# One V tile near the end of a decode step loaded as three row groups instead of one

## The chip, the cores and the metric

The kernel runs on one core of one Trainium2 chip. The core has five instruction streams that matter here: TensorE (PE in the profile, with its weight loads as PEld), VectorE (DVE), ScalarE (ACT), GpSimd (POOL) and SyncE (SP). SyncE issues nearly all transfers; sixteen DMA engines carry them out. The metric is the device time of one execution in microseconds (us). Three timed runs of the kernel before gave 1319.47, 1320.37 and 1320.67 us, so the median is 1320.37 us.

## What is computed

One decode step of a transformer block, two batch entries with one new token each: a layer norm, attention of 32 heads against a cache of 8192 keys and values per head, a residual, a second layer norm, a gated feed-forward network (SwiGLU), and a second residual. All numbers are float32. Cut to what matters, with D = 512, H = 32, Dh = 128, Sk = 8192, F = 1792:

```python
q = (layernorm(x) @ wq).reshape(B, Sq, H, Dh).transpose(0, 2, 1, 3)
scores = einsum("bhqd,bhkd->bhqk", q, k_cache) * Dh ** -0.5
o = einsum("bhqk,bhkd->bhqd", softmax(scores), v_cache)
h = x + o.transpose(0, 2, 1, 3).reshape(B, Sq, H * Dh) @ wo
n = layernorm(h)
out = h + (silu(n @ w_gate) * (n @ w_up)) @ w_down
```

The cache makes up nearly all of the data: 64 pairs of batch entry and head, each with 4 MB of K and 4 MB of V, which is 537 MB of the 565 MB that the kernel reads. Each byte of it is used once.

## The kernel before

**Tiles.** The 64 pairs are numbered i = 2 * head + batch, so NP = 64. A K or V of one pair, 8192 rows of 128 numbers, is laid on the 128 partitions of the on-chip memory so that partition p holds cache rows 64p to 64p + 63: 32 KB in one run per partition. Such a tile is called an item. All items, and the weights too, go through one ring of five buffers of that size (RING = 5).

**The list of loads.** `order` is a list written out before anything is issued. For each pair it has K of that pair and the V's that are due (`after[i]`; V runs behind K, by one pair at first and by five at the end), with wq and wo between them. Behind the last K (pair 63) come V of 58, V of 59, 60 and 61, the last part of wo, V of 62, V of 63 in four pieces, then w_gate, w_up in two pieces and w_down in four (8, 4, 1 and 1 of its 14 column blocks). `NP - 6` is pair 58: the first V behind the last K.

**Issuing.** `pump()` goes down the list and calls `load()` for each piece as soon as the item five places before it in the ring has been used. The `dma_start` at line 120 issues the K and V pieces, line 130 wo, line 136 w_gate and w_up, line 141 w_down, all on SyncE's queue. Each load waits on SyncE until its buffer is free: V of 58 takes the buffer of K of 61, wo's last part that of K of 63, V of 62 that of V of 58.

**Work on a K.** VectorE multiplies the K tile by the broadcast q in two halves (line 245), sums each product over the 128 numbers (line 248), and takes the maximum of its partition (line 256). PE and ScalarE then make the softmax weights `p` (lines 260 to 281).

**Work on a V.** `pv` (line 288) runs 32 matmuls whose stationary side is four columns of `p` and whose moving side is 512 columns of the V tile, so each reads all 128 partitions; it cannot start before the whole tile is there. `epilogue` (lines 301 to 311) folds the result into `oT`, and `project_o` (line 318) multiplies by wo.

**The end.** After V of 63 come the residual `h` (line 376), the layer norm, the gate and up products (line 396), their product `gu` and its transpose `gT` (lines 414 and 420), and 56 matmuls with w_down (line 425, recorded as 112 passes), which read the column blocks of w_down in order. `res` (line 434) is copied out and two small transfers of four rows each store it (line 436), one issued by SyncE and one by ScalarE. The input x is loaded by ScalarE as two rows (line 64).

Of the kernel before, what the change touches and what calls it, by code (L numbers as in the profile page):

```python
# [13 lines left out]
P = 128  # L14
# [5 lines left out]
def tile_decode_block(  # L20
# [12 lines left out]
    nc = tc.nc  # L33
    B, _, D = x.shape
    _, H, S, DH = k_cache.shape
# [10 lines left out]
    NP = B * H  # L46
# [23 lines left out]
    def k_pieces(i):  # L70
        return NCH if i == 0 else 1
# [32 lines left out]
        stream_v(v)  # L104
    order += [(("wg", 0), 0, DC)] + [(("wu", 0), c, 2) for c in range(0, DC, 2)]
    order += [(("wd", 0), c, n) for c, n in ((0, 8), (8, 4), (12, 1), (13, 1))]
    items = list(dict.fromkeys(o[0] for o in order))
    slot = {}
    done = set()
# [2 lines left out]
    def load(item, e, n):  # L112
        if item not in slot:
            slot[item] = ring.tile([P, NJ * DH], F32, name="ring")
        t = slot[item]
        kind, i = item
        if kind in "kv":
            src = k_cache if kind == "k" else v_cache
            h, b = divmod(i, B)
            nc.sync.dma_start(  # L120
                t[:, e * DH : (e + n) * DH],
                src[b, h].rearrange("(p j) d -> p (j d)", p=P)[:, e * DH : (e + n) * DH],
            )
        elif kind == "wq":
            nc.sync.dma_start(
                t[:, : DC * G * DH].rearrange("p (c m) -> p c m", c=DC),
                wq[:, i * G * DH : (i + 1) * G * DH].rearrange("(c p) m -> p c m", p=P),
            )
        elif kind == "wo":
            nc.sync.dma_start(  # L130
                t[:, : G * D].rearrange("p (c m) -> p c m", c=G),
                wo[i * G * DH : (i + 1) * G * DH, :].rearrange("(c p) m -> p c m", p=P),
            )
        elif kind in ("wg", "wu"):
            src = w_gate if kind == "wg" else w_up
            nc.sync.dma_start(
                t[:, e * F : (e + n) * F],
                src.rearrange("(p c) f -> p (c f)", p=P)[:, e * F : (e + n) * F],
            )
        else:  # L140
            nc.sync.dma_start(
                t[:, e * D : (e + n) * D],
                w_down.rearrange("(p c) m -> p (c m)", p=P)[:, e * D : (e + n) * D],
            )

    def pump():
        while state["next"] < len(order):
            piece = order[state["next"]]
            if piece[0] not in slot:
                n = items.index(piece[0])  # L150
                if n >= RING and items[n - RING] not in done:
                    return
            load(*piece)
            state["next"] += 1
# [16 lines left out]
    for n in range(2):  # L171
        t = psum.tile([P, W * DH], F32, name=f"opart{n}")
# [160 lines left out]
    for i in range(NP):  # L333
        n = FINE if k_pieces(i) > 1 else 2 * FINE
# [142 lines left out]
```

## Time and profile before

| what | value |
|---|---|
| median of three timed runs | 1320.37 us (1319.47 to 1320.67) |
| the profiled execution's own time | 1320.22 us |
| its span, first to last instruction | 1318.4 us |
| VectorE busy | 1156.2 us, 88% of the span |
| PE busy | 649.3 us, 49% |
| ScalarE busy | 117.3 us, 9% |
| read from the cache and weights | 564.66 MB, 428 GB/s over the span |
| share of the closing chain put down to DMA | 45% |
| share of the closing chain put down to VectorE | 47% |

The profile is one execution. Its span leaves out 1.8 us of the execution's own time, which lie before the first and after the last instruction. The chain of work that ended last is followed back from the last instruction, at each step to whatever released it. A DMA's "issue to landing" runs from the instruction on the issuing engine to the last of its completions: each DMA engine that takes part in a transfer writes a completion packet of 4 bytes behind its own data, and a waiting engine goes on when all are in. The views count these packets among those under 512 B.

### The profile page before, as it was taken

The page shows a single profiled execution, that of the slowest core. Times are in us where ns is not written, and L with a number is a line of the kernel's source. Part 1 is how long each engine was busy: PE and PEld are TensorE (multiplying, and loading weights), DVE is VectorE, ACT ScalarE, POOL GpSimd, SP SyncE. Part 2 cuts the span into 40 slices and gives each one's busy share as a digit, 9 for nine tenths or more (in the row PEclk, how much of TensorE's full clock was granted, in tenths as well). Part 3 has the DMA queues.
Part 4 walks back from the last instruction along what each step waited for, and adds up shares of the span by engine and source line. Part 5 has one row for each costly group of instructions (what it writes and reads, how often), then busy time and mean ns, then how long its engine had stood idle before and what let it go on. Part 6 is the DMA issues. An engine that isn't in the chain of part 4 may idle for free.

```text
span 1318.4 us, 8048 instructions
## 1 busy us (share of the span) xinstructions
PE 649.3 (49%) x3328; PEld 251.2 (19%) x3328; DVE 1156.2 (88%) x474; ACT 117.3 (9%) x404; POOL 1.9 (0%) x9
## 2 busy tenths in 40 slices
PE   5444544247554435535653454442644754454585
PEld 2111111013212111211221122111212211111122
DVE  6999999997999999989889999997799999999601
ACT  1001000001000100000100000000100000100010
POOL 0000000000000000000000000000000000000000
PEclk9666666677675756666867656666856766666697
DMA  9999999999999999999999999999999999999997
GB/s 404 437 431 428 433 437 433 423 437 432 428 436 435 430 430 435 437 429 429 433 429 434 435 429 431 433 432 435 431 432 426 430 437 432 433 429 435 434 422 327
DMA packets 26633, 565.19 MB, mean 429 GB/s; under 512 B 2394, under 2 KB 2402, under 8 KB 8804
## 3 DMA queue, kind: packets, MB, share of 16 engines
q1 hardware_dynamic: 26584, 564.67, 99.6%
q8 instruction: 26, 0.43, 0.1%
q14 instruction: 11, 0.09, 0.0%
q10 hardware_dynamic: 12, 0.01, 0.0%
HBM read 564.66 MB, written 0.00 MB: 428 GB/s over the span
## 4 chain that ended last, share of the span: by engine, by line
DVE 47%; DMA 45%; PE 7%; issue 0%; ACT 0%; DVEq 0%
DMA ring<-in_A_k_cache_dram 31%; DVE s L248 24%; DVE ring L245 22%; DMA ring<-in_A_v_cache_dram 12%; PE wide L223 4%; DMA ring<-in_B_w_down_dram 2%; PE opart L288 2%; PE attn L318 1%; DMA ring<-in_A_wq_dram 1%; DVE m L256 0%; PE small L425 0%; PE small L304 0%; DVE r L279 0%; PE small L260 0%; DVE gm L264 0%
## 5 line engine op out<-in xcount | busy, mean ns | idle before, releaser
L245 DVE TENSOR_TENSOR ring<-ring,qsb 128x4096 f32<-128x4096 f32 (+1 forms) x130 | 565.4, 4349 | 69.2 <-DMA ring<-in_A_k_cache_dram 56.8
L248 DVE TENSOR_REDUCE s<-ring 128x32 f32<-128x4096 f32 (+1 forms) x130 | 565.0, 4347 | 0.7 <-DVE gm L264 0.5
L288 PE MATMUL opart<-ring,p 128*4 128x512 f32 x2048 | 349.5, 843 | 111.3 <-DMA ring<-in_A_v_cache_dram 111.1
L260 PE MATMUL small<-ident,m 128*1 128x128 f32 x128 | 30.4, 328 | 276.5 <-DVE m L256 276.5
L266 PE MATMUL small<-gm,nscale 1*128 1x1 f32 x128 | 35.8, 346 | 207.7 <-DVE gm L264 207.7
L288 PEld LDWEIGHTS opart<-ring,p 128*4 128x4 f32 x2048 | 57.6, 107 | 346.5 <-issue 228.5
L304 PE MATMUL small<-rdiag,osb 128*128 128x1 f32 x512 | 94.1, 305 | 7.1 <-ACT osb L301 7.1
L304 PEld LDWEIGHTS small<-rdiag,osb 128*128 128x128 f32 x512 | 88.7, 261 | 31.2 <-issue 17.4
L266 PEld LDWEIGHTS small<-gm,nscale 1*128 1x128 f32 x128 | 30.3, 292 | 217.6 <-DVE gm L264 214.9
L260 PEld LDWEIGHTS small<-ident,m 128*1 128x1 f32 x128 | 5.5, 81 | 332.9 <-DVE m L256 330.6
L223 PE MATMUL wide<-ring,xb 128*128 128x512 f32 x128 | 58.4, 616 | 2.9 <-DMA ring<-in_A_wq_dram 2.9
L281 ACT ACTIVATE rdiag<-diag,r 128x4 f32<-128x4 f32 x64 | 19.0, 297 | 451.4 <-DVE r L279 451.4
L275 PE MATMUL small<-rs,ones 128*128 128x1 f32 x128 | 36.1, 351 | 46.9 <-ACT p L271 46.9
L264 DVE TENSOR_REDUCE gm<-small 1x1 f32<-1x128 f32 x64 | 17.4, 272 | 34.1 <-PE small L260 34.1
L301 ACT ACTIVATE osb<-opart 128x512 f32<-128x512 f32 x64 | 37.8, 590 | 88.9 <-PE opart L288 88.8
L275 PEld LDWEIGHTS small<-rs,ones 128*128 128x128 f32 x128 | 30.6, 297 | 52.4 <-ACT p L271 52.4
L268 ACT ACTIVATE nb<-small 128x1 f32<-128x1 f32 x64 | 11.0, 172 | 290.4 <-PE small L266 290.0
L318 PE MATMUL attn<-ring,oT 128*2 128x512 f32 x64 | 36.7, 734 | 0.3 <-ACT oT L311 0.3
L311 ACT ACTIVATE oT<-small 128x1 f32<-128x1 f32 x64 | 11.0, 171 | 277.3 <-PE small L304 277.3
L223 PEld LDWEIGHTS wide<-ring,xb 128*128 128x128 f32 x128 | 24.9, 197 | 35.8 <-issue 35.8
L376 DVE TENSOR_TENSOR h<-attn,xs 2x512 f32<-2x512 f32 x1 | 0.7, 678 | 30.5 <-PE attn L318 30.5
L271 ACT ACTIVATE p<-s,nb 128x64 f32<-128x64 f32 x64 | 22.2, 347 | 2.1
(43 smaller groups left out, 87.7 us busy)
## 6 DMA issues: line engine op xcount, KB each, us to landing
ring<-in_A_k_cache_dram SPq DMA_DIRECT2D x63, 4096.0 KB, 31.4
ring<-in_A_v_cache_dram SPq DMA_DIRECT2D x63, 4096.0 KB, 30.5
ring<-in_A_wq_dram SPq DMA_DIRECT2D x4, 2048.0 KB, 21.4
ring<-in_A_wo_dram SPq DMA_DIRECT2D x4, 2048.0 KB, 27.9
ring<-in_A_k_cache_dram SPq DMA_DIRECT2D x4, 1024.0 KB, 12.3
ring<-in_A_v_cache_dram SPq DMA_DIRECT2D x4, 1024.0 KB, 22.3
ring<-in_B_w_gate_dram SPq DMA_DIRECT2D x1, 3584.0 KB
ring<-in_B_w_up_dram SPq DMA_DIRECT2D x2, 1792.0 KB, 37.2
```

The costliest lines, as they stand in the source:

```text
L223: nc.tensor.matmul(ps, xb[:, c * B + b, :], w[:, c, n : n + 512], start=(c == 0), stop=(c == DC - 1),)
L245: nc.vector.tensor_tensor(kt, kt, qb, op=OP.mult)
L248: nc.vector.tensor_reduce(st[i]["s"][:, j0 : j0 + n], k_view(i, j0, n), axis=AX.X, op=OP.add)
L260: nc.tensor.matmul(st[i]["mrow"], st[i]["m"], ident, start=True, stop=True)
L266: nc.tensor.matmul(nb_ps, nscale, gm, start=True, stop=True)
L271: nc.scalar.activation(st[i]["p"], st[i]["s"], AF.Exp, bias=nb, scale=SCALE, accum_out=rs)
L275: nc.tensor.matmul(st[i]["den"], ones, rs, start=True, stop=True)
L281: nc.scalar.activation(st[i]["r"], diag, AF.Copy, scale=r)
L288: nc.tensor.matmul(o[32 * t : 32 * t + W, :], st[i]["p"][:, w * W : (w + 1) * W], vt[:, w * W * DH : (w + 1) * W * DH], start=(w < 4), sto ...
L301: nc.scalar.activation(osb, opart[i % 2], AF.Copy)
L304: nc.tensor.matmul(ot_ps, osb[:, a * DH : (a + 1) * DH], st[i]["r"][:, a : a + 1], start=(a == 0), stop=(a == W - 1),)
L318: nc.tensor.matmul(attn, oT[:, h, :], w[:, h - g * G, :], start=(h == 0), stop=(h == H - 1))
```

## The change

The list `order`, the ring and all work on the tiles stay as they are. V of pair 58 is issued as three transfers in a row on SyncE's queue instead of one: rows (partitions) 0 to 111, rows 112 to 119 and rows 120 to 127, each with the full 32 KB per row. Together they fill the same buffer with the same bytes. The matmuls that read the tile depend on all three. All other K and V loads still run the loop once, over 128 rows.

```diff
     order += [(("wd", 0), c, n) for c, n in ((0, 8), (8, 4), (12, 1), (13, 1))]
+
+    SHARED = ((0, 112), (112, 8), (120, 8))
+    shared = {("v", NP - 6)}
     items = list(dict.fromkeys(o[0] for o in order))
...
             h, b = divmod(i, B)
-            nc.sync.dma_start(
-                t[:, e * DH : (e + n) * DH],
-                src[b, h].rearrange("(p j) d -> p (j d)", p=P)[:, e * DH : (e + n) * DH],
-            )
+            rows = src[b, h].rearrange("(p j) d -> p (j d)", p=P)
+            for r0, nr in SHARED if item in shared else ((0, P),):
+                nc.sync.dma_start(
+                    t[r0 : r0 + nr, e * DH : (e + n) * DH],
+                    rows[r0 : r0 + nr, e * DH : (e + n) * DH],
+                )
```

## The prediction

> **What bounds the kernel now.** I begin with the page's row of the DMA engines in 40 slices and with its table of queues (packets, MB, share of sixteen engines' time).
>
> ```profile
> DMA  9999999999999999999999999999999999999997
> ...
> q1 hardware_dynamic: 26584, 564.67, 99.6%
> q8 instruction: 26, 0.43, 0.1%
> q14 instruction: 11, 0.09, 0.0%
> q10 hardware_dynamic: 12, 0.01, 0.0%
> ```
>
> All sixteen engines are busy until the last slice. Nearly all of it is queue q1, SyncE's loads; beside it run 37 fetches of program code (q8 and q14). Next comes the view by stretches of time, whose last two columns are the DMA share and GB/s: first a long steady stretch, then the end cut finely.
>
> ```profile
> 120.00:1200.00 1080.00, 520.19 (x2572) 202.18 (x2564) 1004.94 (x393) 95.64 (x341) 0.00 (x0) 0.66 1.00 432
> ...
> 1296.00:1307.00 11.00, 8.54 (x74) 2.38 (x73) 0.79 (x2) 0.54 (x1) 0.00 (x0) 0.81 1.01 429
> ...
> 1309.20:1310.20 1.00, 0.00 (x0) 0.00 (x0) 0.00 (x0) 0.00 (x0) 0.00 (x0) 0.50 0.64 270
> ...
> 1310.40:1312.00 1.60, 1.60 (x32) 1.60 (x36) 0.00 (x0) 0.00 (x0) 0.00 (x0) 0.50 0.54 215
> 1312.00:1312.60 0.60, 0.60 (x20) 0.60 (x16) 0.00 (x0) 0.00 (x0) 0.00 (x0) 0.50 0.22 82
> 1312.60:1313.50 0.90, 0.90 (x24) 0.90 (x20) 0.00 (x0) 0.00 (x0) 0.00 (x0) 0.50 0.06 25
> 1313.50:1313.90 0.40, 0.40 (x20) 0.40 (x16) 0.00 (x0) 0.00 (x0) 0.00 (x0) 0.83 0.01 5
> ```
>
> The steady rate is 432 GB/s, 27.0 per engine, so one row of 32,768 bytes occupies an engine for 32,768 / 27.0e3 = **1.21 us**. That is the change's unit. The end shows that the sixteen do not finish together. A share of 0.64 is ten engines of sixteen, so six are done by 1309.2; 0.54 is nine, so a seventh ends near 1310.2; eight end between 1312.0 and 1312.6; 0.06 is one, and it ends at about 1313.6. Every engine has the same loads, so the late nine are late by something else. The spread is there already at the V in question, whose sixteen completions (the packets under 512 B) fall into three neighbouring windows, 1229.05 to 1230.3, to 1231.7 and to 1233.1:
>
> ```profile
> DMA packets 23, 0.56 MB, mean 446 GB/s; under 512 B 6, under 2 KB 6, under 8 KB 6
> ...
> DMA packets 23, 0.69 MB, mean 492 GB/s; under 512 B 2, under 2 KB 2, under 8 KB 2
> ...
> DMA packets 29, 0.69 MB, mean 492 GB/s; under 512 B 8, under 2 KB 8, under 8 KB 8
> ```
>
> Six, two, eight: a spread of 4 us between first and last engine. Code fetches are the likely cause: 26 fetches of 16 KB that always fall on the same engines push these back. Last, the chain of work that ended last, from the end of the K work on (start, length, what):
>
> ```profile
> 1222.14 55.33 DMA ring<-in_A_v_cache_dram x2
> 1277.52 3.66 PE opart L288 x32
> 1281.19 29.07 DMA ring<-in_B_w_down_dram
> 1310.39 4.86 PE small L425 x112
> 1315.28 0.29 DVE res L434
> ```
>
> The last 93 us are transfers with two short PE pieces between them. w_down's first piece lands at 1281.19 + 29.07 = 1310.26, PE starts at 1310.39 and runs without a stop to 1315.25, so its other three pieces are in time. **The end is set by the slowest of sixteen engines at w_down's first piece.** That engine has 1313.6 - 1310.26 = 3.3 us of load behind it. The others have the same behind theirs, so they have that piece in 3.3 us before they end: the eight at 1308.7 to 1309.3, the seventh at 1306.9, the six by 1305.9.
>
> **The change part by part.** *Issue.* SyncE's timeline around the load has these rows:
>
> ```profile
> 1202.68 0.80 SPq L120 DMA_DIRECT2D ring<-in_A_v_cache_dram  x2
> ...
> 1222.14 0.80 SPq L120 DMA_DIRECT2D ring<-in_A_v_cache_dram  x2
> ```
>
> V of 58 and V of 59 are issued within 0.80 us, then SyncE waits until 1222.14 for a buffer. Two more issues at about 0.4 us each end near 1204.3. V of 59, the only load queued behind them, comes 0.8 us later, and its data are not due before 1229, when V of 58's first completions come. Price nothing; without that cover 0.8 us.
>
> *Wait.* The 32 matmuls of V of 58 now wait for three transfers.
>
> ```profile
> 1233.39 6.15 PE L288 MATMUL opart<-ring,p 128*4 128x512 f32 x32 [3.12 <-DMA ring<-in_A_v_cache_dram]
> ...
> 1241.47 0.38 SPq L130 DMA_DIRECT2D ring<-in_A_wo_dram  x1
> 1241.94 17.54 SPq L120 DMA_DIRECT2D ring<-in_A_v_cache_dram  x1
> ...
> 1243.18 6.37 PE L288 MATMUL opart<-ring,p 128*4 128x512 f32 x32 [1.86 <-DMA ring<-in_A_v_cache_dram]
> ```
>
> Behind them on PE stand pair 58's epilogue and V of 59's matmuls (1243.18), and on SyncE the load of V of 62, which takes V of 58's buffer. That load's issue is held 17.54 us with its engines full of earlier work. A landing some microseconds later than 1233 makes V of 62's issue begin later inside that hold, and moves V of 59's matmuls by a little; the next thing the transfers wait for is far off. Price nothing; that cover would be gone only for a delay of over ten microseconds.
>
> *Rows per engine.* 128 rows on sixteen engines are eight each, 112 are seven. How a load of fewer rows than engines is split shows in q10: it carries x's two rows and one store of four rows, and its 12 packets are just (2 + 2) + (4 + 4), one data packet and one completion for each row, so one engine for each row. An eight-row load then occupies eight engines, with one row each. Two of them on the same eight give these 7 + 1 + 1 = nine rows and leave the others with seven: **eight engines gain 1.21 us of work and eight lose 1.21 us.** All engines are full to the end, so the shift stays until w_down.
>
> The single-packet records behind the views, which no view prints, put x's two rows on engines of the early group; if the engines are always filled from the same end, the eight that gain work are mostly the early ones. [...]
>
> *Sum.* The early ones are seven, and the half that gains has eight, so one of the nine late engines is in it too. The very last, if it is in the half that loses, has w_down's first piece at 1310.26 - 1.21 = 1309.05. The late one in the half that gains has it at 1308.7 to 1309.3 plus 1.21, so 1309.9 to 1310.5: it takes over the end. The change comes to **-0.4 to +0.2 us; I take -0.1**. More than 1.3 us cannot be had in any case, since the other operand is not ready earlier:
>
> ```profile
> 1308.38 0.65 DVE L420 STREAM_TRANSPOSE gT<-gu 128x448 f32<-128x448 f32 x1
> ```
>
> It ends at 1309.03 against PE's start at 1310.39.
>
> *Unknown: several engines at neighbouring rows.* In a load of 128 rows each engine has rows of its own; in the short ones eight engines write eight neighbouring rows at once, and none of the rows above shows such writes. [...] If each engine keeps its rate, nothing. [...] I take nothing, nearest to the steady row, where 432 GB/s hold over 1080 us, and keep the other end as a rival.
>
> **Rivals.** [...]
>
> [...]
>
> *Wrong half.* If the eight that gain hold the last engine, w_down's first piece lands at 1310.26 + 1.21: +1.2, **1321.6 us**. For it: the views do not number the engines. Against it: x's two rows.
>
> *It does not do what it says.* If the short loads are spread so that each engine still gets the same bytes, nothing moves: **1320.4 us**. Against it: the twelve packets of q10.
>
> **How the numbers follow.** The sum is made against the profiled execution, 1320.22 us with a span of 1318.4; the median of the runs shown is 1320.37, 0.15 above it, and I move that median. Forecast: 1320.37 - 0.1 = 1320.3 us, its own range 1319.9 to 1320.6. Two runs of this kernel can be told apart from about 0.2%, 2.6 us. Chances: the forecast 0.42; shared way 0.40, of which 0.27 lies beyond +2.6; wrong half 0.08; nothing moved 0.05; a mishap in issue or waits that costs over 2.6 us 0.02; a gain of over 2.6 us, which the operand gT excludes by all I see, 0.03. So faster 0.03, same 0.42 + 0.13 + 0.08 + 0.05 = 0.68, slower 0.27 + 0.02 = 0.29. The range goes from 1319.3 (the forecast's lower end less the spread of the runs) to 1324.8 (the shared way up to +4.4), leaving out about one in ten.
>
> **What would show it.** V of 58 with 48 completions less the unused ones (16 + 8 + 8 = 32 packets) confirms the split. Forecast right: w_down's first piece lands within 0.5 us of 1310.3, the six early engines end 1.2 us later, most of the late eight 1.2 us earlier, so the step in the DMA share near 1312 moves to about 1311. [...] Wrong half: the last engine ends near 1314.8. I am wrong altogether if the end no longer hangs on w_down's first piece, or if engines stand idle before 1308.

## The result, and the profile after

The changed kernel took 1335.19 us (median of four runs, 1334.64 to 1336.48) against 1319.96 us for the kernel before (median of four: the three runs above and one more). The ratio is 1.0115 with a 95% interval of 1.0102 to 1.0127: **15.2 us slower**. The forecast was 1320.3 us and its range ended at 1324.8. Both are far off.

The page of the changed kernel, rows of the DMA engines and queues, in the same 40 slices:

```profile
span 1334.7 us, 8052 instructions
...
DMA  9999999999999999999999999999999999999997
GB/s 408 427 438 431 432 435 429 436 428 438 424 438 427 439 428 436 429 435 428 436 426 437 430 434 437 428 435 430 436 429 431 433 432 432 435 429 340 316 426 325
DMA packets 26649, 565.19 MB, mean 423 GB/s; under 512 B 2410, under 2 KB 2418, under 8 KB 8820
...
q1 hardware_dynamic: 26600, 564.67, 99.6%
```

The engines are as busy as before, but in slices 37 and 38 they move 340 and 316 GB/s instead of some 430. The bytes are the same. The profiled execution is the slowest of the four (1336.48 us), 16.3 us above the profiled one of the kernel before. Queue q1 has 26,600 packets against 26,584, sixteen more: V of 58 now has 16 + 8 + 8 completions instead of 16, so the split is carried out as intended. Where the rate falls is seen in the view by stretches (the last two columns are DMA share and GB/s). First the kernel before:

```profile
1218.00:1224.00 6.00, 3.00 (x26) 1.25 (x18) 4.63 (x3) 0.84 (x3) 0.00 (x0) 0.99 1.01 437
1224.00:1235.00 11.00, 2.77 (x12) 1.25 (x16) 11.00 (x4) 0.61 (x3) 0.00 (x0) 0.54 0.99 429
1235.00:1251.00 16.00, 12.68 (x75) 3.43 (x67) 6.66 (x4) 1.66 (x4) 0.00 (x0) 0.68 1.01 433
1251.00:1300.00 49.00, 36.02 (x217) 10.92 (x221) 2.82 (x8) 5.53 (x15) 0.54 (x1) 0.83 1.01 427
```

The same stretches of the changed kernel:

```profile
1218.00:1224.00 6.00, 2.35 (x22) 1.11 (x14) 4.32 (x2) 0.82 (x3) 0.00 (x0) 0.97 1.08 273
1224.00:1235.00 11.00, 1.16 (x4) 0.99 (x4) 6.88 (x3) 0.61 (x3) 0.00 (x0) 0.50 1.03 220
1235.00:1251.00 16.00, 0.00 (x0) 0.00 (x0) 11.08 (x5) 0.30 (x1) 0.00 (x0) 0.50 0.97 203
1251.00:1300.00 49.00, 37.12 (x213) 10.40 (x213) 0.45 (x2) 5.95 (x15) 0.00 (x0) 0.83 1.00 425
```

For 33 us, 1218 to 1251, the sixteen engines run at **half rate with a full busy share**, and then at full rate again. In these 33 us they move 437 x 6 + 429 x 11 + 433 x 16 = 14.3 MB before and 273 x 6 + 220 x 11 + 203 x 16 = 7.3 MB after. The missing 7.0 MB take 16.1 us at 432 GB/s, and the span grew by 16.3, from 1318.4 to 1334.7. That is nearly the whole loss of this execution.

The slow stretch reaches loads that were not touched. VectorE's timeline at the first half of K of 63, whose load was issued ahead of V of 58, shows how long it had to wait in the kernel before

```profile
1223.71 4.42 DVE L245 TENSOR_TENSOR ring<-ring,qsb 128x4096 f32<-128x4096 f32 x1 [1.34 <-DMA ring<-in_A_k_cache_dram]
```

and in the changed one:

```profile
1228.12 4.42 DVE L250 TENSOR_TENSOR ring<-ring,qsb 128x4096 f32<-128x4096 f32 x1 [5.77 <-DMA ring<-in_A_k_cache_dram]
```

A plain load of 128 rows lands 4.4 us late. The rate falls about when the first engines go on to the split load, while others are still in K of 63: six of its sixteen completions are in by 1220.4, the other ten come from 1223.9 to 1227.2, and in the kernel before these ten came from 1221.3 to 1223.4. The end of the closing chain after (start, length, what; pieces of under 0.2 us are left out):

```profile
1203.52 48.56 DMA ring<-in_A_v_cache_dram
1252.22 6.39 PE opart L293 x32
1258.63 36.93 DMA ring<-in_A_v_cache_dram
1295.61 3.66 PE opart L293 x32
1299.28 0.33 SPq L146
1299.66 30.00 DMA ring<-in_B_w_down_dram
1329.71 1.75 PE small L430 x48
1331.48 0.29 DVE res L439
```

V of 58 lands near 1252.1 instead of 1233. Behind it all stays as it was, only later. w_down's second piece now ends last: PE starts on the first and then stands for 0.40 us. The sixteen engines end further apart than before, from a DMA share of 0.90 in 1322 to 1324 down to 0.18 in 1328 to 1330, and that they do is the likely reason.

### The profile page after: what moved, and what is told of

It reads as the page before. It is cut to its first block, busy times and chain, and to the rows that moved or that the text cites. A ratio compares the mean times of both kernels' runs of the same rounds, so it can differ in the third digit from the quotient of the medians.

```text
span 1334.7 us, 8052 instructions
## 1 busy us (share of the span) xinstructions
PE 650.7 (49%) x3328; PEld 252.5 (19%) x3328; DVE 1156.4 (87%) x474; ACT 117.1 (9%) x404; POOL 1.9 (0%) x9
## 3 DMA queue, kind: packets, MB, share of 16 engines
q1 hardware_dynamic: 26600, 564.67, 99.6%
## 4 chain that ended last, share of the span: by engine, by line
DVE 46%; DMA 46%; PE 7%; issue 0%; ACT 0%; SPq 0%; DVEq 0%
DMA ring<-in_A_k_cache_dram 29%; DVE s L253 23%; DVE ring L250 22%; DMA ring<-in_A_v_cache_dram 14%; PE wide L228 4%; DMA ring<-in_B_w_down_dram 2%; PE opart L293 2%; PE attn L323 1%; DMA ring<-in_A_wq_dram 1%; DVE m L261 0%; PE small L309 0%; DVE gm L269 0%; DVE r L284 0%; PE small L265 0%; PE small L430 0%
## 5 line engine op out<-in xcount | busy, mean ns | idle before, releaser
L309 PE MATMUL small<-rdiag,osb 128*128 128x1 f32 x512 | 97.1, 311 | 7.0 <-ACT osb L306 7.0
L309 PEld LDWEIGHTS small<-rdiag,osb 128*128 128x128 f32 x512 | 91.6, 269 | 31.6 <-issue 17.9
L273 ACT ACTIVATE nb<-small 128x1 f32<-128x1 f32 x64 | 10.9, 171 | 291.6 <-PE small L271 291.2
```

The lines of the kernel that those rows point to most:

```text
L309: nc.tensor.matmul(ot_ps, osb[:, a * DH : (a + 1) * DH], st[i]["r"][:, a : a + 1], start=(a == 0), stop=(a == W - 1),)
```

## The experiments

Each run is one timed execution beside one of the kernel before on the same chip, with a profile. All executions of the kernel before lie between 1319.47 and 1321.61 us; the one beside e1 to e4 is the slowest of them, so the losses of these four may be up to 1.5 us larger than the table says. A difference of under some 3 us between two runs is not read as one. "Place" means the rows that one engine has in a load of 128 rows; no view says which they are.

| run | V of 58 is loaded as | us | before | difference |
|---|---|---|---|---|
| e1_112_16 | 112, 16 rows | 1331.97 | 1321.61 | +10.4 |
| e2_64_64 | 64, 64 | 1332.81 | 1321.61 | +11.2 |
| e3_32x4 | 32, 32, 32, 32 | 1333.71 | 1321.61 | +12.1 |
| e4_pair30 | 112, 8, 8, for V of 30 | 1333.73 | 1321.61 | +12.1 |
| e5_32_64_32 | 32, 64, 32 | 1331.60 | 1320.11 | +11.5 |
| e6_16_16_64_32 | 16, 16, 64, 32 | 1332.09 | 1320.11 | +12.0 |
| e7_step4 | 32, four times 16 four apart, 32 | 1331.00 | 1320.11 | +10.9 |
| e8_8step2 | 112, twice 8 two apart | 1335.75 | 1320.11 | +15.6 |
| f1_from5 | 128, read from five rows on | 1320.55 | 1320.20 | +0.4 |
| f2_stride2 | 128, every second row read | 1319.47 | 1320.20 | -0.7 |
| f3_onerow_64 | 64, 64, one row read | 1331.86 | 1320.20 | +11.7 |
| f4_onerow_128 | 128, one row read | 1320.12 | 1320.20 | -0.1 |
| g1_mid_step4 | rows 32 to 95 only, four times 16 four apart | 1315.57 | 1320.08 | -4.5 |
| g2_mid_64 | rows 32 to 95 only, one load | 1315.62 | 1320.08 | -4.5 |
| g3_mid_16x4 | rows 32 to 95 only, four times 16 neighbours | 1324.21 | 1320.08 | +4.1 |
| g4_low8 | rows 0 to 31 only, four times 8 four apart | 1314.46 | 1319.50 | -5.0 |
| g5_high8 | rows 96 to 127 only, four times 8 four apart | 1322.88 | 1319.50 | +3.4 |

### Which part of the split costs, and where

```diff
-    SHARED = ((0, 112), (112, 8), (120, 8))
+    SHARED = ((0, 112), (112, 16))                       # e1_112_16
+    SHARED = ((0, 64), (64, 64))                         # e2_64_64
+    SHARED = ((0, 32), (32, 32), (64, 32), (96, 32))     # e3_32x4
...
-    shared = {("v", NP - 6)}
+    shared = {("v", 30)}                                 # e4_pair30
```

Theory A is that every part of fewer than 128 rows costs transfer rate; theory B is that the two parts of eight rows alone do, so that nearly all of the loss would be gone without them, within 3 us. By theory A the author's estimate for twice 64 rows and for four times 32 is +9.7 us (8 to 14): eight rows per engine at 2.43 us, twice the 1.21 us of the steady rate.

> V of 58 as rows 0 to 111 and rows 112 to 127: seven rows and one row on every engine, so no engine has more than before. Theory A (whichever transfer is not 128 rows puts several engines on the same ways into the memory, and the 112-row part is the worst of it because it is the longest): still slow, +9 to +15 us over the kernel before. [...]

> V of 58 as twice 64 rows, four rows on each engine each time. [...] Theory B, and a theory C by which only a row count that does not divide the 128 rows evenly disturbs: within 2 us of the kernel before.

> V of 58 as four times 32 rows, two rows on each engine each time. [...] If the loss goes with the number of transfers instead, twice that of the two halves. Theories B and C: within 2 us of the kernel before.

> The changed kernel's split (112, 8, 8) moved from V of 58 to V of 30, in the middle. If the loss is one of DMA throughput alone it is the same here, +14 to +17 us, since the engines are full from here to the end. If it comes from what stands near the end (the late start of V of 62's load, a wait of PE on three transfers), it is under 3 us.

112 and 16 rows give every engine eight rows as before by the count (7 + 1), with no eight-row load at all, and still cost 10.4 us. So theory B falls: the two short loads account for the other 4.8 of the 15.2. The rates say the same: e1 moved 339, 238 and 292 GB/s from 1218 to 1224, 1235 and 1251, where the kernel before moved 437, 429 and 433, so by the sum above 11.4 us are missing there and 16.1 in the changed kernel. Row counts that divide 128 evenly cost the same (11.2 and 12.1), so theory C falls, and so does a price per transfer, for four transfers cost about as much as two. With V of 30 the loss is 12.1, a little under the 14 to 17 that were expected, so it does not come from the end of the kernel: there it is a loss of transfer rate too, 229 GB/s in the 27 us from 643 to 670. Theory A stands as far as the loss goes (why several engines would hinder each other is not shown), but the size already looks odd: 112 rows and 32 rows lose about the same. The stretch from 1220 to 1244 with 112 and 16 rows and then with twice 64:

```profile
1220.00:1244.00 24.00, 3.77 (x18) 2.87 (x14) 19.42 (x8) 1.68 (x6) 0.00 (x0) 0.56 1.02 233
```

```profile
1220.00:1244.00 24.00, 2.53 (x14) 2.05 (x14) 19.23 (x8) 1.58 (x6) 0.00 (x0) 0.61 1.00 220
```

Both are about half rate: the last number hardly depends on how many rows a load has.

### Each load by itself: a theory that fell

```diff
-    SHARED = ((0, 112), (112, 8), (120, 8))
+    SHARED = ((0, 32), (32, 64), (96, 32))               # e5_32_64_32
+    SHARED = ((0, 16), (16, 16), (32, 64), (96, 32))     # e6_16_16_64_32
...
-            for r0, nr in SHARED if item in shared else ((0, P),):
+            for r0, nr, dr in SHARED if item in shared else ((0, P, 1),):
+                r1 = r0 + (nr - 1) * dr + 1
                 nc.sync.dma_start(
-                    t[r0 : r0 + nr, e * DH : (e + n) * DH],
-                    rows[r0 : r0 + nr, e * DH : (e + n) * DH],
+                    t[r0:r1:dr, e * DH : (e + n) * DH],
+                    rows[r0:r1:dr, e * DH : (e + n) * DH],
                 )
...
+    SHARED = ((0, 32, 1), (32, 16, 4), (33, 16, 4), (34, 16, 4), (35, 16, 4), (96, 32, 1))  # e7_step4
+    SHARED = ((0, 112, 1), (112, 8, 2), (113, 8, 2))     # e8_8step2
```

Theory S is the author's guess that each load loses rate by itself, by which rows of the on-chip memory it writes: neighbouring rows lose, while rows four apart and rows 32 to 95 do not. No run up to here shows it. The author's estimates by it are +5 to +6 us for 32, 64 and 32 rows, about half of the 11.2 us of twice 64; 4.9 us more (four rows of 1.21 us) with the first 32 rows in sixteens; and with step four the same as 32, 64 and 32 rows, within 1.5 us.

> V of 58 as rows 0 to 31, rows 32 to 95 and rows 96 to 127. [...] Theory H (any load of fewer than 128 rows halves the rate, or it is the reads of the cache that clash): +10 to +12 us as with twice 64 rows, which reads the same bytes in pieces of the same kind.

> As the kernel with 32, 64 and 32 rows, but the first 32 rows as two loads of 16 neighbouring rows. [...] Theory H: half rate whatever the load, so no more than with 32, 64 and 32 rows, within 1.5 us of it.

> As the kernel with 32, 64 and 32 rows, but the middle 64 rows as four loads of 16 rows that lie four apart (32, 36, ... 92 and so on). [...] A theory by which short loads as such cost (few rows, one packet per engine, more completions): at least 5 us more than with 32, 64 and 32 rows.

> The changed kernel, but the two loads of eight rows take every second row (112, 114, ... 126 and 113, 115, ... 127), so that each reaches four groups of four rows instead of two; the same eight engines have the same rows. Theory S: the part of the loss that the 8-row loads add to the 112 rows (15.2 - 10.4 = 4.8 us by the runs so far) shrinks to half or less: +11 to +13 us over the kernel before. If the ways play no part in it: +14 to +16 us as the changed kernel.

Theory S counted each load by itself. By the times it missed three of the four. 32, 64 and 32 rows lost 11.5 us and not 5 to 6; the first 32 rows in sixteens added 0.5 and not 4.9; eight-row loads with rows two apart lost 15.6 and not 11 to 13. Only the loads with step four came out as expected beside their neighbour (10.9 against 11.5). By the numbers theory H, "any load of fewer than 128 rows halves the rate", was ahead at this point. But its second half, that reads clash, was still untried, and the step-four kernel did not fit the first half. Around 1230, when the single packets show nearly all engines inside the step-four loads, rows took 1.22 to 1.87 us, and before and after that about 2.4; with its mix of loads that run could not show it clean.

The rates of e8 are kinder to theory S than its time. From 1218 to 1224, 1235 and 1251 it moved 317, 229 and 252 GB/s, so by the sum above 13.5 us are missing there: over e1's 11.4 the short loads add 2.1 us, where those of the changed kernel add 4.7. Another 1.3 us of e8's loss lie behind the transfers, for PE's last 112 passes took 6.14 us instead of 4.86. Whether spreading the short loads helps is therefore not settled by this one execution.

### Reads or writes

```diff
-    SHARED = ((0, 112), (112, 8), (120, 8))
+    SHARED = ((0, P),)                                   # f1, f2, f4
+    SHARED = ((0, 64), (64, 64))                         # f3
...
             rows = src[b, h].rearrange("(p j) d -> p (j d)", p=P)
+            if item in shared:                           # f1, f2
+                every = src.rearrange("b h (p j) d -> (b h p) (j d)", p=P)
+                rows = every[(b * H + h) * P + 5 : (b * H + h) * P + 5 + P, :]    # f1
+                rows = every[(b * H + h) * P : (b * H + h) * P + 2 * P : 2, :]    # f2
+            if item in shared:                           # f3, f4
+                rows = rows[0:1, :].to_broadcast([P, NJ * DH])
```

> V of 58 as one load of 128 rows, but read from five rows further on in the cache (it reads 123 rows of V of 58 and five of its neighbour, so the values of that pair are others). Where each engine writes is as before; which rows are read together relative to the loads before and behind is not. Theory W (engines clash where they write): full rate, within 1 us of the kernel before. Theory R (engines clash where they read): half rate, +8 to +13 us.

> V of 58 as one load of 128 rows, read from every second row of the cache from V of 58's start (half of the rows are its neighbour's, so the values of that pair are others). Theory W: full rate, within 1 us of the kernel before. Theory R: the rows that are read together lie twice as far apart, half rate or worse, +8 us or more.

> V of 58 as twice 64 rows, all of them read from the first row of that V (its other rows are not read). Theory W: the same loss as twice 64 rows, +10 to +12 us. Theory R: another result than that and about the same as one load of 128 rows from one row.

> V of 58 as one load of 128 rows, all of them read from the first row of that V (its other rows are not read): the control of the kernel with twice 64 rows from one row. Theory W: full rate, within 1 us of the kernel before, unless one row read by sixteen engines is slow in itself. Theory R: slow, and about as slow as twice 64 rows from one row.

This settles one side. 128 rows run at full rate whatever they read: shifted by five rows, every second row, or one row 128 times (+0.4, -0.7, -0.1 us). Twice 64 rows lose 11.7 us even when all of them read the same row, as much as with their own rows (11.2). The same stretch with one row read, as one load of 128 and then as twice 64:

```profile
1220.00:1244.00 24.00, 10.01 (x58) 4.08 (x62) 20.54 (x9) 2.08 (x8) 0.00 (x0) 0.66 1.00 432
```

```profile
1220.00:1244.00 24.00, 3.84 (x18) 2.86 (x14) 19.48 (x8) 1.68 (x6) 0.00 (x0) 0.55 1.03 227
```

Theory R falls. **What is left is where the engines write**, or the short load as such, which the next runs tell apart.

### Fewer rows, or rows in the wrong place

The last five load only a part of the rows, so that no other part can disturb; GpSimd sets the rest to 0, and is done with it before 1218.

```diff
-    SHARED = ((0, 32, 1), (32, 16, 4), (33, 16, 4), (34, 16, 4), (35, 16, 4), (96, 32, 1))
+    SHARED = ((32, 16, 4), (33, 16, 4), (34, 16, 4), (35, 16, 4))      # g1
+    SHARED = ((32, 64, 1),)                                            # g2
+    SHARED = ((32, 16, 1), (48, 16, 1), (64, 16, 1), (80, 16, 1))      # g3
+    SHARED = ((0, 8, 4), (1, 8, 4), (2, 8, 4), (3, 8, 4))              # g4
+    SHARED = ((96, 8, 4), (97, 8, 4), (98, 8, 4), (99, 8, 4))          # g5
...
             rows = src[b, h].rearrange("(p j) d -> p (j d)", p=P)
+            if item in shared:
+                nc.gpsimd.memset(t[0:32, :], 0.0)        # g1 to g3; g4: 32:64, 64:128
+                nc.gpsimd.memset(t[96:128, :], 0.0)      # g5: 0:64, 64:96
```

Theory W1 is that a load is harmless if each engine writes in the place that it has in a load of 128 rows, and that the rate halves where engines do not. The author's estimate by it for g1 is -3 to -6 us, around the 4.85 us that four rows of 1.21 us are worth.

> Of V of 58 only rows 32 to 95 are loaded, by four loads of 16 rows that lie four apart (GpSimd sets the other rows to 0, so half of that pair's values are left out). That is four rows per engine instead of eight, 4.85 us less at full rate. [...] Theory W2 (any load of fewer than 128 rows halves the rate wherever it writes): four rows at half rate on top of the mixing with the neighbours' loads, 0 to +6 us.

> The same rows 32 to 95 by one load of 64 rows, the rest as there. Theory W1 with consecutive shares (engine k has rows 32 + 4k to 35 + 4k): the same as the four loads with step four, -3 to -6 us. W1 with the shares dealt out in another way, or W2: 0 to +6 us.

> The same rows 32 to 95 by four loads of 16 neighbouring rows, the rest as there; it differs from the first of these three only in which rows go together. Theory W1: sixteen engines in four groups of four rows at once, half rate or worse: +2 to +15 us against the kernel before, and at least 5 us over the four loads with step four. Theory W2: the same as the four loads with step four, within 1.5 us.

> Of V of 58 only rows 0 to 31 are loaded, by four loads of eight rows that lie four apart (0, 4, ... 28 and so on; GpSimd sets the other rows to 0, so three quarters of that pair's values are left out). Eight engines have four rows, each in the place that it has in a 128-row load; the other eight have none. W1: full rate. The eight with four rows lose 4.85 us of work and the others 9.7, so -4.5 to -7 us against the kernel before. W2: the rate halves while the loads run, 0 to +4 us.

> The same with rows 96 to 127 (96, 100, ... 124 and so on): the same eight engines with the same number of rows, but in the places of the other eight, which at that time write there with their own loads before and behind. W1: clash, at least 3 us over the kernel with the low rows, and packets of 2 us and more also on engines that have no row of it. W2: the same as with the low rows, within 1.5 us.

g1 and g3 load the same 64 rows by four loads of sixteen, one row per engine and load. With rows four apart the kernel gains 4.5 us, close to the 4.85 that half the rows are worth; with neighbouring rows it loses 4.1. Their stretches from 1220 to 1234, g1 and then g3:

```profile
1220.00:1234.00 14.00, 7.13 (x42) 3.06 (x38) 12.64 (x6) 1.38 (x5) 0.00 (x0) 0.63 0.99 428
```

```profile
1220.00:1234.00 14.00, 1.70 (x15) 1.22 (x12) 8.06 (x5) 0.77 (x2) 0.00 (x0) 0.68 1.05 229
```

So few rows per load do no harm as such, and theory W2 falls. g2 does the same in one load of 64 at 422 GB/s, as theory W1 had it with consecutive shares; which engine has which rows no view shows. g4 and g5 make the point with the change's own tool, eight-row loads, the same number of them and the same number of rows. Their rates:

```profile
1220.00:1234.00 14.00, 7.31 (x42) 3.61 (x42) 12.59 (x6) 1.38 (x5) 0.00 (x0) 0.63 0.99 428
```

```profile
1220.00:1234.00 14.00, 1.94 (x12) 1.55 (x12) 8.18 (x5) 0.61 (x4) 0.00 (x0) 0.64 0.98 206
```

In the low rows the kernel gains 5.0 us at full rate, in the high rows it loses 3.4 at half rate. In g5 the slow packets are not those of the split load alone: from 1220 to 1234 the engines together move 206 GB/s, and the single packets behind the view, those of K of 63 and V of 59 among them, all take 2.4 to 2.6 us.

**What the runs show is this.** Three splits leave the rate as it is: rows 32 to 95 in one load of 64 rows (422 GB/s), the same rows in four loads of sixteen rows four apart (428), and rows 0 to 31 in four loads of eight rows four apart (428). With every other split that was tried, sixteen neighbouring rows (229) and eight rows four apart in rows 96 to 127 (206) among them, the sixteen engines together go at about half rate, in the changed kernel until V of 58 lands near 1252. The rate is much the same in all such runs, 202 to 242 GB/s over the slow stretch.

One reading fits all of them. It is the author's inference, for no view numbers the engines or says which rows one of them writes: each engine has its place in a 128-row load, and a load of fewer rows is harmless where every engine writes in its own place; where engines write in others' places, all sixteen are slowed. By this reading the fewest engines out of place that were tried are the eight of g5. It also fits what theory S missed: in 32, 64 and 32 rows the early engines begin the first 32 while the late ones are still in K of 63, and the late ones end the last 32 after the early ones have gone on to V of 59, so the slow stretch covers most of the harmless 64 as well; only near 1230 do the rows of that kernel get shorter, 1.36 to 1.82 us. That the rate is a half, for sixteen neighbouring rows (229 GB/s) as for 64 (220), is not explained: theory S had the former slower, as an estimate. Why all sixteen engines slow down was not tried.

## Why the prediction was wrong

**What bounds the kernel: right in kind, wrong in the piece.** The end still hangs on w_down's landing (1299.66 + 30.00 = 1329.66, PE's last start at 1329.71), and a loss of transfer rate reaches the end in full: 16.1 us worked out from the rates against 16.3 in the span. But it is now the second piece, and not the first, by 0.40 us. This is one of the two signs that I had set for being wrong altogether; the account of transfers as the limit stands all the same.

**Issue: right.** SyncE issued the three parts and V of 59 by 1204.3; the slow stretch begins 14 us later.

**Wait: right in its outcome, too narrow in its cover.** V of 58's matmuls started 18.8 us later and V of 62's load was issued 16.7 us later, more than the ten microseconds that I allowed. Neither let the engines run empty: from 1251 to 1300 they moved 425 GB/s against 427 before. The whole stream had slipped with them.

**Rows per engine: right as a count.** Sixteen more completions show 16 + 8 + 8. Which engines gain is another matter. The sum takes the eight that gain to be the seven early ones and a single late one. In g4 loads of eight rows, as in the change, give rows of V of 58 to eight engines and none to the other eight, so the completions of V of 59 come in two groups. The eight without rows have theirs by 1233.1 (2, 2 and 4 of them from 1230 to 1231.2, 1232.5 and 1233.1), and the eight with rows theirs by 1238.0 (4, 2 and 2 from 1234.3 to 1235.5, 1237.2 and 1238.0). Without the four rows, 4.85 us, the last of the second group would stand with the last of the first. So in that execution both halves had early and late engines, and the latest were in both. The shift of 1.2 us may as well have moved the end the other way; under a loss of 15 us no run shows it.

**The step that failed** is "Unknown: several engines at neighbouring rows": *"I take nothing, nearest to the steady row, where 432 GB/s hold over 1080 us"*. That row is made of 128-row loads alone. It says nothing about another assignment of rows to engines, and it should not have been taken as the nearest row to one. The measured price is half rate for 33 us, 16.1 us of transfer in the profiled execution.

**The shared way**, the slower rival among the chances (0.40), sets the end of the range with its +4.4 us. No run shows the term behind it. What the runs showed in its place is half rate on all sixteen engines, through V of 58 and through what each of them has in front of and behind it: 7.0 MB too few in 33 us, 16.1 us at 432 GB/s. The two eight-row loads are not the larger part of it, for the split into 112 and 16 rows loses 10.4 of the 15.2 us. The eight rows of V of 58 at half rate are 9.7 us, an estimate from 1.21 us per row, and the rest is the neighbours' loads. V of 58 landed 19 us late, its rows took 2.1 to 3.6 us by the single packets, and the rate fell to between 203 and 273 GB/s. So the direction of this rival came true, and its size did not.

**It does not do what it says** did not occur. **Wrong half** is open, as said above.

## What to carry to other kernels

Before a 128-row load is cut by rows, ask which rows each part writes, not only how many bytes each engine gets: here the cut into 112, 8 and 8 rows halved the rate of all transfers in flight, from 429 to 220 GB/s between 1224 and 1235, while the DMA share read 1.03. Cuts along the row (fewer columns of all 128 rows) did no such harm: V of 63 comes in four such pieces, in a stretch that ran at 427 GB/s before. Nor did rows 32 to 95 in one load, at 422 GB/s. When a price is bounded by "nothing", look whether the row that speaks for nothing contains the new situation at all.

## What the runs showed of the hardware that was not expected

- A full busy share does not mean full rate: from 1224 to 1235 the share was 1.03 at 220 GB/s, against 0.99 at 429 before.
- The half rate is nearly the same for 112, 64, 32, 16 and 8 rows per load (202 to 242 GB/s), and it spreads to loads that were issued earlier: K of 63 came 4.4 us late in the changed kernel.
- Reading one row of the cache 128 times costs nothing and gains nothing: 432 GB/s from 1220 to 1244, as with 128 different rows (432 in f1 and f2, 434 before).
